# Rests of the kv sums on row halves, one PSUM ring for q and k products, loads as steps of a newly ordered list

## The chip, the cores and the metric

One core of one Trainium2 chip runs the kernel. The metric is the device time of one execution in microseconds (us), as the median of several runs.

## The reference

Linear attention over 8 batches of 8 heads (576 tokens, 64 dimensions) feeds a mixture of 8 experts that picks one expert per token.

```python
def phi(x):                                   # x: q or k, (8, 8, 576, 64)
    proj = np.einsum('bhsd,df->bhsf', x, w_phi)          # 128 features
    proj = proj - np.max(np.abs(proj), axis=-1, keepdims=True)
    return np.concatenate([np.exp(proj), np.exp(-proj)], axis=-1)
kv = np.einsum('bhsf,bhsd->bhfd', k_p, v); z = np.sum(k_p, axis=2)
num = np.einsum('bhsf,bhfd->bhsd', q_p, kv)
den = np.einsum('bhsf,bhf->bhs', q_p, z)[..., None] + 1e-06
...                                           # x = num / den as (4608, 512)
logits = x @ w_gate + modality_bias[modality_id]
e_idx = np.argmax(logits, axis=1)             # one expert per token
...                                           # gate_w: softmax at e_idx
out[mask] = gate_w[mask, None] * (np.maximum(x[mask] @ w1[e], 0.0) @ w2[e])
```

## The kernel before, in words

The work comes in two stages. **Attention** runs over 16 groups `qi` of four heads. Each group goes through the units K, Q, V, T, N and L, and each unit is a Python generator whose `yield`s cut it into steps:

- **K0, K1, K2** (`k`, L550): products of k with w_phi for four, four and one tiles of 128 tokens, two products side by side on the row halves of the array (64 rows, 128 columns of weights; L565); then the largest absolute value (VectorE, L569), the subtraction (L574), two exponentials (ScalarE, L580). The results lie in a PSUM tile of the ring `pk`, which has one slot.
- **Q0, Q1** (`q`, L583): two pairs of products each (L592) into the ring `pq`, also of one slot, a copy each (ScalarE, L596), a maximum over partitions (GpSimd, L600), the subtraction (VectorE, L603), two exponentials (L609).
- **V** (`v`, L612): the kv sums, for the two signs `s` in turn. Of a head's 576 tokens, 512 lie in eight tiles `va` of 128 rows (two row blocks of four); the 64 left over of two heads share one tile, zero-padded in `vb`. The rests (L621) multiply the shared tile with `vb`, 130 columns wide; the main part (L625) is 65 columns wide. Both split the 128 columns of weights into two halves of 64 that run side by side.
- **T** (`t`, L635): four transposes (L641), a copy, products with the gate weights (L650). **N0 to N3, L** (`n`, `l`): numerators and denominators (L676, L695), the division on VectorE, a store of x through SP.

After two `qi` a batch's routing can go on: `xr` and `xl` sum the logits, and **R** (`r`, `Route.group`, L221) finds for four or five tiles of tokens the expert, its weight and the token's place in the expert's list: ten small VectorE operations, a rank product on TensorE (L260, L263), then seven more. **E** and **F** plan the first expert slots from 27 of the 36 tiles.

**Experts** (from p = 0) gather 256 tokens a slot, transpose them, multiply by weights split in a high and a low part (casts L829, L831), and scatter. The first two slots (M, S, MM, SS, L866 and L903) are steps of the same list, with the splits of the weights (W, Y, U); from p = 2 on, `slots` writes fixed code (L883, L885, L903).

**What sets the order.** `ORDER` (L1082) is a written-out list of 1153 steps. TensorE, ScalarE, VectorE and SP take their instructions in the list's order; GpSimd follows dependences and a chain of places (`Line`). Loads aren't in the list: seven stand ahead of it, and `step` (L1187) issues the load for `qi + 2` once the reads of `qi` counted in `READS` have been issued. Ahead of everything, `Numbers`, `Route`, `Attention` and `values` issue their constants: memsets, a running count over 128 columns, a partition number by a product (L99), an identity, 12 and 16 products on ones that keep TensorE at work (L88, L102).

Of the kernel before, what the change touches and what calls it, by code (L numbers as in the profile page):

```python
# [7 lines left out]
F32 = mybir.dt.float32  # L8
# [10 lines left out]
P = 128  # L19
# [18 lines left out]
WARM2 = 16  # L38
# [36 lines left out]
class Numbers:  # L75


    def __init__(self, tc, c, w, ps):
        nc = tc.nc
        self.one = w.tile([P, P], BF16, name="one", bufs=1)  # L80
        nc.vector.memset(self.one, 1.0)

# [3 lines left out]
        pw = ps.tile([P, 512], F32, tag="pm", name="warm")  # L86
        for _ in range(WARM):
            nc.tensor.matmul(pw[:, 0:256], self.one, self.one.unsqueeze(1).to_broadcast([P, 2, P]), start=True, stop=True)  # L88
        self.free = w.tile([P, P], F32, name="free", bufs=1)
        nc.vector.memset(self.free[:, 0:1], 0.0)  # L90
        n = 1
# [3 lines left out]

        mean = w.tile([P, 8], F32, name="mean", bufs=1)
        nc.vector.memset(mean, 1.0 / P)
        pp = ps.tile([P, 512], F32, tag="pm", name="numbers")[:, 0:8]
        nc.tensor.matmul(pp, self.free, mean, start=True, stop=True)  # L99
        pw = ps.tile([P, 512], F32, tag="pm", name="warm2")  # L100
        for _ in range(WARM2):
            nc.tensor.matmul(pw[:, 0:256], self.one, self.one.unsqueeze(1).to_broadcast([P, 2, P]), start=True, stop=True)  # L102
        self.part = w.tile([P, 1], F32, name="partition", bufs=1)
        nc.vector.tensor_copy(self.part, pp[:, 0:1])
        self.ident = c.tile([P, P], F32, name="ident")
        nc.vector.tensor_scalar(self.ident, self.free, self.part, None, ALU.is_equal)
        self.U = w.tile([P, P], BF16, name="U", bufs=1)
        nc.vector.tensor_scalar(self.U, self.free, self.part, None, ALU.is_gt)


class Route:


    def __init__(self, tc, c, w, num, mod, bias, lst):
        self.tc, self.nc, self.lst, self.c, self.w = tc, tc.nc, lst, c, w
        self.listed, self.U = [], num.U
        nc = tc.nc
        self.m2 = w.tile([P, NT, 2], I32, name="m2", bufs=1)
        nc.scalar.dma_start(self.m2, mod.bitcast(I32).rearrange("p (t w) -> p t w", w=2))
        self.bb = w.tile([P, 2, E], F32, name="bb", bufs=1)  # L120
        nc.scalar.dma_start(self.bb, bias.rearrange("m e -> (m e)").partition_broadcast(P)
                            .rearrange("p (m e) -> p m e", m=2))

        self.pad = w.tile([P, E * CAP // P, 2], I32, name="pad", bufs=1)

        self.k = c.tile([P, MOST], F32, name="kf")
        nc.vector.tensor_copy(self.k, num.free[:, 0:MOST])
        self.e = self.k[:, :E]
        self.w8 = c.tile([P, E], F32, name="w8")
        nc.vector.tensor_scalar(self.w8, self.e, -1.0, float(E), ALU.mult, ALU.add)  # L130
        self.ecap = c.tile([P, E], F32, name="ecap")
        nc.vector.tensor_scalar(self.ecap, self.e, float(CAP), None, ALU.mult)
        self.base = c.tile([P, E], F32, name="base")
        nc.vector.tensor_copy(self.base, self.ecap)
        self.k256, self.k32 = (c.tile([P, n], F32, name=f"k{s}") for n, s in ((MOST, 256), (UM, UR)))
        nc.vector.tensor_scalar(self.k256, self.k, 256.0, None, ALU.mult)
        nc.vector.tensor_scalar(self.k32, self.k[:, :UM], float(UR), None, ALU.mult)
        self.row = w.tile([P, P], BF16, name="row", bufs=1)
        nc.vector.tensor_copy(self.row, num.free)
        self.one = num.one  # L140

        self.oh = [c.tile([P, T + 1, E], BF16, name=f"oh{T}") for T in (4, 5)]
        for t in self.oh:
            nc.vector.memset(t, 0.0)

        idf = w.tile([P, NT // 9, 9], F32, name="idf", bufs=1)
        g = w.tile([P, NT // 9], F32, name="first", bufs=1)
        t = w.tile([P, 4], F32, name="tile", bufs=1)
        nc.vector.tensor_scalar(g, num.free[:, 0:NT // 9], 2.0 * S, num.part, ALU.mult, ALU.add)
        nc.vector.tensor_scalar(t, num.free[:, 0:4], float(P), None, ALU.mult)  # L150
        sh = [P, NT // 9, 4]
        nc.vector.tensor_tensor(idf[:, :, 0:4], g.unsqueeze(2).to_broadcast(sh), t.unsqueeze(1).to_broadcast(sh), ALU.add)
        nc.vector.tensor_scalar(idf[:, :, 4:8], idf[:, :, 0:4], float(S), None, ALU.add)
        for j in range(2):
            r = slice(64 * j, 64 * j + 64)
            nc.vector.tensor_scalar(idf[r, :, 8], g[r], float(512 + j * (S - 64)), None, ALU.add)
        self.meta = c.tile([P, NT, 2], F32, name="meta")
        nc.vector.tensor_copy(self.meta.bitcast(I32)[:, :, 1], idf.rearrange("p g t -> p (g t)"))
        self.idf = idf.rearrange("p g t -> p (g t)")[:, :ET]
# [5 lines left out]
        self.me = c.tile([P, 2 * EARLY, 2], I32, name="me")  # L165

# [53 lines left out]

    def group(self, lg, T0, T, pm):  # L221

        nc, w = self.nc, self.w
        sh = [P, T, E]
        n = f"{T0}"
        l = w.tile([P, 5, E], F32, tag="l", name="l" + n)[:, :T]
        nc.vector.tensor_tensor(l, lg, self.bias[:, T0:T0 + T], ALU.add)
        yield
        mx = w.tile([P, 5], F32, tag="mx", name="mx" + n)[:, :T]
# [4 lines left out]
        ex = w.tile([P, 5, E], F32, tag="ex", name="ex" + n)[:, :T]  # L234
# [3 lines left out]
        sc = w.tile([P, 5, E], F32, tag="sc", name="sc" + n)[:, :T]  # L238
# [4 lines left out]
        ohz = self.oh[T - 4]  # L243
# [5 lines left out]
        sm = w.tile([P, 5], F32, tag="sm", name="sm" + n)[:, :T]  # L249
# [29 lines left out]
        lo = self.c.tile([P, 5], I32, tag="lor", name="lor" + n, bufs=2)[:, :T]  # L279
# [4 lines left out]
        for t in range(T0, T0 + T):  # L284
            nc.vector.tensor_scalar(self.low[:, t], self.row, self.lof[:, t:t + 1], None, ALU.is_equal)
# [195 lines left out]
class Attention:  # L481
# [3 lines left out]
    def __init__(self, tc, c, num, w_phi, w_gate):  # L485
        self.tc, self.nc, self.ident = tc, tc.nc, num.ident
        nc = tc.nc
        self.st, self.gs, self.gl, self.lg = {}, {}, {}, {}

        self.wp = c.tile([P, P], F32, name="wp")  # L490
        nc.scalar.dma_start(self.wp[0:64], w_phi)
        nc.scalar.dma_start(self.wp[64:P], w_phi)
        first = c.tile([P, 1], F32, name="first")
        nc.vector.memset(first, 0.0)
        nc.scalar.activation(first, first, AF.Exp)

        self.wgb = c.tile([P, 4, 16], F32, name="wgb")
        nc.vector.memset(self.wgb, 0.0)
        self.wg = w_gate.rearrange("(p j d) e -> j d p e", j=2, d=64)
        self.fold = c.tile([P, 64], F32, name="fold")  # L500
        nc.vector.tensor_tensor(self.fold, self.ident[:, 0:64], self.ident[:, 64:P], ALU.add)

    def values(self, lv):

        nc = self.nc

        self.va = [lv.tile([P, 2, 4, 130], F32, name=f"va{i}") for i in range(2)]
        self.vb = [lv.tile([P, 2, 130], F32, name=f"vb{i}") for i in range(2)]
        for i in range(2):
            nc.vector.memset(self.va[i][:, :, :, 0:130:129], 1.0)  # L510
            nc.vector.memset(self.vb[i], 0.0)
            for j in range(2):
                nc.vector.memset(self.vb[i][64 * j:64 * j + 64, j, 0:130:129], 1.0)
# [6 lines left out]
    def load_q(self, qi, ld, qT, js=(slice(0, 2),)):  # L520
        nc, q = self.nc, self.st.setdefault(qi, {})
        qv = qT[qi].rearrange("p (r a) s -> p a r s", a=2)
        if "qt" not in q:
            q["qt"] = ld.tile([P, 2, S], F32, tag="qt", name=f"qt{qi}")
        for j in js:
            for a in range(2):
                r = slice(64 * a, 64 * a + 64)
                nc.sync.dma_start(q["qt"][r, j], qv[r, a, j])
# [829 lines left out]
```

## Time and profile before

| | us |
|---|---|
| median of 3 runs | 710.33 (710.23 to 710.48) |
| the profiled execution | 710.49 |
| its span, first to last instruction | 708.7 |
| TensorE busy in the span | 695.4 |
| VectorE busy | 555.2 |
| ScalarE busy | 447.1 |
| GpSimd busy | 273.4 |

Engines: PE is TensorE, PEld its weight loads, DVE VectorE, ACT ScalarE, POOL GpSimd, SP the queue that issues most DMAs. A float32 product shows as two records, so a pair of products side by side is four. Ends of matrix products are modelled and overlap the next start, so lengths of TensorE's steps are best read where a chain of waits runs along the engine, from start to start. A line of a chain, as `45.16 0.69 PE pq L592 x4`, is start, length, engine, tile, line of the kernel and number of records.

### The profile page before, as it was taken

To read this page: it belongs to the slowest core of one execution; us is meant where nothing else is said; L and a number is where in the kernel's file an instruction comes from. 1 tells how busy PE (TensorE), PEld (TensorE's weight loads), DVE (VectorE), ACT (ScalarE), POOL (GpSimd) and SP (SyncE) were. 2 spreads that over 40 slices of the span, in tenths; PEclk is the share of its full clock that TensorE was granted. 3 is DMA by queue.
4 is the path that set the end of the run, shared out by engine and by line. 5 is a ranking of instruction groups with operands and counts; after the bars stand their busy time and mean duration, and the time that the engine had idled before them with its cause. 6 is when DMAs were issued, how large, how long until landed. Compare 5 with 4: busy or idle time off the path is not lost.

```text
span 708.7 us, 21200 instructions
## 1 busy us (share of the span) xinstructions
PE 695.4 (98%) x8670; PEld 601.4 (85%) x8670; DVE 555.2 (78%) x1287; ACT 447.1 (63%) x739; POOL 273.4 (39%) x157
## 2 busy tenths in 40 slices
PE   7999999999999999999999999999999999999996
PEld 5889888899898899988888888878888888888885
DVE  7888879899999988679997786678467477578762
ACT  4888688787985884346755575557347357357651
POOL 3555446555545732377733312231231231222021
PEclk9999999999999999999999999999999999999998
DMA  8655555555654658575667549996988983585410
GB/s 231 161 156 162 159 151 152 140 156 158 168 151 127 203 200 283 176 280 176 204 224 290 200 142 412 417 416 224 390 329 336 379 293 132 207 296 191 177 75 28
DMA packets 69705, 155.07 MB, mean 219 GB/s; under 512 B 16090, under 2 KB 44894, under 8 KB 57824
## 3 DMA queue, kind: packets, MB, share of 16 engines
q1 hardware_dynamic: 61920, 134.60, 56.2%
q0 software_dynamic: 7232, 18.92, 7.3%
q8 instruction: 70, 1.15, 0.7%
q14 instruction: 35, 0.29, 0.1%
q10 hardware_dynamic: 448, 0.11, 0.1%
HBM read 134.90 MB, written 19.55 MB: 218 GB/s over the span
## 4 chain that ended last, share of the span: by engine, by line
PE 77%; issue 10%; DVE 5%; POOL 2%; ACT 1%; DMA 1%; SPq 0%; POOLq 0%; ACTq 0%
PE p L903 18%; PE p L883 12%; PE pn L676 9%; PE pv L625 7%; PE p L885 6%; PE pq L592 5%; PE pk L565 4%; PE p L866 3%; DVE l L831 2%; PE pv L621 2%; PE pt L839 2%; PE pt L903 2%; PE pt L1037 1%; PE up L1023 1%; POOL out_dram L791 1%
## 5 line engine op out<-in xcount | busy, mean ns | idle before, releaser
L831 DVE TENSOR_TENSOR l<-raw,h 128x1024 fp32r<-128x1024 f32 x144 | 172.5, 1218 | 5.3 <-ACT h L829 5.2
L600 POOL PARTITION_ALL_REDUCE mq<-d x32 | 131.3, 4103 | 115.1 <-ACT d L596 89.7
L829 ACT CAST h<-raw 128x1024 fp32r<-128x1024 f32 x144 | 145.5, 1051 | 3.7 <-PE pt L903 2.2
L883 PE MATMUL p<-xx,h 128*128 128x512 f32 x512 | 140.2, 395 | 0.0
L886 ACT COPY ts<-p 128x256 f32<-128x256 f32 x128 | 47.8, 373 | 108.6 <-PE p L885 108.6
L903 PE MATMUL p<-h,hh 128*128 128x512 f32 x272 | 107.3, 395 | 0.0
L903 PE MATMUL p<-h,hl 128*128 128x512 f32 x272 | 106.1, 390 | 0.0
L903 PE MATMUL p<-l,hh 128*128 128x512 f32 x272 | 106.0, 390 | 0.0
L883 PEld LDWEIGHTS p<-xx,h 128*128 128x128 f32 x512 | 88.1, 189 | 14.1 <-issue 1.8
L887 DVE TENSOR_TENSOR ts<-ts,p 128x256 f32<-128x256 f32 x128 | 53.5, 418 | 59.1 <-ACT ts L886 59.1
L787 POOL DMA_INDIRECT xg<-x,me x36 | 43.5, 1209 | 141.5 <-PE pt L839 73.1
L791 POOL DMA_INDIRECT out_dram<-os,me x36 | 47.6, 1321 | 124.3 <-DVE os L972 81.3
L885 PEld LDWEIGHTS p<-xx,l 128*128 128x128 f32 x512 | 78.6, 189 | 11.8 <-DVE l L831 0.9
L885 PE MATMUL p<-xx,l 128*128 128x256 f32 x512 | 81.7, 281 | 0.7 <-DVE l L831 0.7
L580 ACT ACTIVATE kp<-dk 128x1024 f32<-128x1024 f32 (+1 forms) x96 | 74.7, 837 | 6.4 <-DVE dk L574 6.4
L676 PE MATMUL pn<-kv,qp 128*64 128x73 f32 x2048 | 73.6, 227 | 0.4 <-DVE kv L653 0.4
L676 PEld LDWEIGHTS pn<-kv,qp 128*64 128x64 f32 x2048 | 68.2, 136 | 5.6 <-issue 2.8
L609 ACT ACTIVATE qp<-d 128x1152 f32<-128x1152 f32 x64 | 71.0, 1160 | 1.6 <-DVE d L603 1.3
L625 PE MATMUL pv<-va,kp 128*64 128x65 f32 x2048 | 70.6, 221 | 0.9 <-issue 0.9
L625 PEld LDWEIGHTS pv<-va,kp 128*64 128x64 f32 x2048 | 68.6, 137 | 1.0 <-issue 1.0
L596 ACT COPY d<-pq 128x576 f32<-128x576 f32 x64 | 40.7, 637 | 32.6 <-PE pq L592 31.6
L889 ACT ACTIVATE hh<-ts 128x256 fp32r<-128x256 f32 x128 | 54.3, 424 | 10.6 <-DVE ts L887 10.3
(240 smaller groups left out, 1101.8 us busy)
## 6 DMA issues: line engine op xcount, KB each, us to landing
raw<-in_w_dram SPq DMA_DIRECT2D x92, 1024.0 KB, 7.6
qt<-in_qT_dram SPq DMA_DIRECT2D x30, 288.0 KB, 4.4
va<-in_vm_dram SPq DMA_DIRECT2D x16, 512.0 KB, 5.0
x<-xs SPq DMA_DIRECT2D x64, 128.0 KB, 3.5
kt<-in_kT_dram SPq DMA_DIRECT2D x15, 512.0 KB, 4.3
kt<-in_kT_dram SPq DMA_DIRECT2D x16, 64.0 KB, 4.7
vb<-in_vt_dram SPq DMA_DIRECT2D x32, 32.0 KB, 4.4
x<-xl SPq DMA_DIRECT2D x32, 32.0 KB, 2.8
```

The lines of the kernel that those rows point to most:

```text
L580: nc.scalar.activation(kp[:, 4 * u:4 * u + T, :, s, :].rearrange("p t a f -> p a t f"), dk, AF.Exp, scale=sc)
L600: self.line.put(nc.gpsimd.partition_all_reduce(mq.rearrange("p a s -> p (a s)"), d.rearrange("p a s -> p (a s)"), P, bass_isa.ReduceOp.abs ...
L609: nc.scalar.activation(qp[:, 2 * pr:2 * pr + 2, i, :], d, AF.Exp, scale=sc)
L625: nc.tensor.matmul(pt[c:c + CW, k // 4, a], kp[:, k, a, s, c:c + CW], va[:, k // 4, k % 4, h], start=False, stop=k == 7, tile_position=(0, c))
L676: nc.tensor.matmul(pp[c:c + CW, g], q["qp"][:, g, s, P * j + c:P * j + c + CW], q["kv"][:, s, g // 2, 73 * (g % 2):73 * (g % 2) + 73], sta ...
L791: ins = self.nc.gpsimd.indirect_dma_start(self.out.rearrange("n (h d) -> (n h) d", d=cols), IndirectOffsetOnAxis(ix.bitcast(U32), 0), o, None,
L829: nc.scalar.copy(h, r)
L831: nc.vector.tensor_tensor(l, r, h, ALU.subtract)
L883: nc.tensor.matmul(pp, h1[:, cc, f], self.XX[:, cc].rearrange("p a t -> p (a t)"), start=cc == 0, stop=False)
L885: nc.tensor.matmul(pp[:, 0:256], l1[:, cc, f], self.XH[:, cc], start=False, stop=cc == 3)
L889: a = nc.scalar.activation(self.HH[:, j], s, AF.Relu)
L903: nc.tensor.matmul(pp, a[:, f, tk], b[:, f], start=i == 0, stop=i == 23)
```

## The change

- The rests: `vb` goes. The leftover 64 rows of each head lie in the ninth tile of `va`, and a product for each row half (64 rows, 128 columns of weights, 65 moving columns) writes its own PSUM tile. The rests of both signs become the first step of V; the main part follows by row block `r`, no longer by sign.
- The ring `pk` goes; `pq` has two slots and serves both k and q.
- `Route.group` takes nine tiles at once: R.3, R.7, R.11 and R.15 are left, and the 27 comparisons that fill `low` become three.
- Constants and set-up become steps (NU, NA, NR); of the products on ones, 12 stay ahead of the list, and PI steps issue four more each, with 64 rows.
- Every load is a step of the list (LP, LA, LB, LK, LQ, LV, LG, LM), on SP except half of w_phi. `READS` goes.
- The list is a new one, of 1200 steps.

```diff
-        for s in range(2):
-            pt = pm.tile([P, 512], F32, tag="pm", name=f"pv{n}_{s}")[:, 0:260].rearrange("p (r a c) -> p r a c", r=2, a=2)
-            for a in range(2):
-                h = slice(65 * a, 65 * a + 65)
-                for c in range(0, P, CW):
-                    nc.tensor.matmul(pt[c:c + CW, :, a], kp[:, 8, a, s, c:c + CW], vb[:, :, h],
-                                     start=True, stop=False, tile_position=(0, c))
...
+        for s in range(2):
+            for a in range(2):
+                for r in range(2):
+                    i = slice(64 * r, 64 * r + 64)
+                    nc.tensor.matmul(pt[r][:, s, a], kp[i, 8, a, s], va[i, 8, 65 * a:65 * a + 65],
+                                     start=s + a == 0, stop=False)
+        yield
+        for r in range(2):
+            for s in range(2):
+                for a in range(2):
+                    for k in range(4):
+                        for c in range(0, P, CW):
+                            nc.tensor.matmul(pt[r][c:c + CW, s, a], kp[:, 4 * r + k, a, s, c:c + CW],
+                                             va[:, 4 * r + k, 65 * a:65 * a + 65],
+                                             start=False, stop=s + a + k == 5, tile_position=(0, c))
+            yield
...
-            pv = [pk.tile([P, 2, 4, P], F32, tag="pk", name=f"pk{n}_{u}")[:, :, 0:T]]
+            pv = [pq.tile([P, 2, 512], F32, tag="pq", name=f"pq{n}_{u}").rearrange("p a (t f) -> p a t f", f=P)[:, :, 0:T]]
...
-        pk = pool(pr, "pk", "right", space=PSUM)
-        pq = pool(pr, "pq", "right", space=PSUM)
+        pq = pool(pr, "pq", "right", bufs=2, space=PSUM)
...
+    def idle(self, n, rows=P):
+        pw = self.ps.tile([P, 512], F32, tag="pm", name="idle")
+        for _ in range(n):
+            self.nc.tensor.matmul(pw[:, 0:256], self.one[:rows], self.one[:rows].unsqueeze(1).to_broadcast([rows, 2, P]), start=True, stop=True)
...
+                if u == "PI":
+                    num.idle(qi, 64)
...
-        for t in range(T0, T0 + T):
-            nc.vector.tensor_scalar(self.low[:, t], self.row, self.lof[:, t:t + 1], None, ALU.is_equal)
+        nc.vector.tensor_tensor(self.low[:, T0:T0 + T], self.row.unsqueeze(1).to_broadcast([P, T, P]),
+                                self.lof[:, T0:T0 + T].unsqueeze(2).to_broadcast([P, T, P]), ALU.is_equal)
```

The new list begins so; behind this stretch, PI.4 stands eight more times (ahead of T.4, between Q1.6 and L.5, between N0.8 and L.8, twice around K0.14, on either side of W1.0 and W3.0, ahead of XV1.0):

```
LA.0 LP.0 NU.0 NU.0 K0.0 NA.0 NA.0 NA.0 NU.0 PI.4 LQ.0 PI.4 Q0.0 LB.0 PI.4 NU.0 Q0.0 PI.4 LK.1 K0.0 K2.0 Q0.0 Q0.0
NA.0 K0.0 Q1.0 K2.0 NU.0 Q1.0 LV.0 K1.0 Q1.0 LG.0 K2.1 NU.0 NU.0 NU.0 NU.0 K2.0 K2.0 K1.0 V.0 Q1.0 K0.0 K0.1 K1.0
K1.0 NU.0 LQ.1 V.0 V.0 Q0.0 V.0 K2.1 K0.1 K0.1 K1.1 LV.1 K2.1 Q0.0 LK.2 K0.1 K1.1 Q1.0 NU.0 Q0.1 NU.0 K2.1 K1.1 Q0.0
LV.2 V.0 V.1 V.1 T.0 ...
```

## Rows read from the trace of the kernel before

**Rows 1.** The page's busy time of TensorE, its share of the span, its instructions

```profile
PE 695.4 (98%) x8670; PEld 601.4 (85%) x8670; DVE 555.2 (78%) x1287; ACT 447.1 (63%) x739; POOL 273.4 (39%) x157
```

**Rows 2.** Busy time by stage: PE, PEld, DVE, ACT, POOL, granted clock, DMA share, GB/s

```profile
0.00:10.00 10.00, 8.56 (x54) 6.13 (x56) 5.82 (x44) 1.49 (x2) 2.16 (x9) 1.00 0.71 206
10.00:20.00 10.00, 7.49 (x110) 5.44 (x108) 9.93 (x11) 8.30 (x12) 7.18 (x2) 1.00 1.13 273
...
80.00:100.00 20.00, 19.07 (x457) 17.03 (x455) 14.96 (x34) 15.86 (x24) 8.25 (x3) 1.00 0.48 134
100.00:120.00 20.00, 19.67 (x460) 17.65 (x458) 18.77 (x64) 16.52 (x25) 12.15 (x3) 1.00 0.52 143
220.00:240.00 20.00, 19.62 (x453) 16.91 (x448) 19.70 (x63) 14.87 (x21) 15.07 (x6) 1.00 0.45 127
260.00:280.00 20.00, 19.72 (x261) 19.04 (x262) 16.25 (x36) 11.61 (x17) 6.06 (x6) 1.00 0.95 338
```

**Rows 3.** The chain of waits, 290 to 420 us

```profile
300.68 0.14 PE rk L263 x10
...
312.75 0.91 PE p L883 x4
...
371.88 10.93 PE p L903 x48
...
394.89 10.93 PE p L903 x48
```

**Rows 4.** The chain of waits along TensorE, 44 to 63 us

```profile
45.16 0.69 PE pq L592 x4
...
46.89 0.49 PE pq L592 x4
...
53.06 0.22 PE pk L565 x4
53.28 0.37 PE pv L621 x4
53.66 0.93 PE pv L625 x32
54.59 0.23 PE pv L621 x4
...
56.43 0.89 PE pk L565 x16
...
60.37 0.43 PE kvT L650 x16
```

**Rows 5.** TensorE's weight loads by line and shape, before 312 us

```profile
L625 PEld LDWEIGHTS pv<-va,kp 128*64 128x64 f32 x2048 | 68.6, 137 | 1.0 <-issue 1.0
...
L565 PEld LDWEIGHTS pk<-wp,kt 64*128 64x128 f32 x576 | 38.3, 188 | 9.1 <-issue 2.5 <-DVE dk L574 1.7 <-PE pq L592 1.6
```

**Rows 6.** TensorE in order of time, before 24 us: start, length, group

```profile
4.62 3.57 PE L102 MATMUL warm<-one 128*128 128x256 bf16 x16
8.13 1.65 PE L565 MATMUL pk<-wp,kt 64*128 64x128 f32 x20
...
23.50 0.76 PE L592 MATMUL pq<-qt,wp 64*128 64x288 f32 x4
```

**Rows 7.** DMA issues: number, KB each, median us to landing

```profile
kt<-in_kT_dram SPq DMA_DIRECT2D x2, 256.0 KB, 3.2
...
wp<-in_w_phi_dram ACTq DMA_DIRECT2D x2, 32.0 KB, 3.1
```

**Rows 8.** VectorE by line and shape, before 312 us: busy us, mean ns

```profile
L574 DVE TENSOR_TENSOR dk<-pk,mk 128x1024 f32<-128x1024 f32 x31 | 37.8, 1220 | 0.9
...
L230 DVE TENSOR_REDUCE mx<-l 128x5 f32<-128x40 f32 x4 | 0.8, 196 | 0.1
```

**Rows 9.** ScalarE by line and shape, before 312 us

```profile
L580 ACT ACTIVATE kp<-dk 128x1024 f32<-128x1024 f32 x64 | 63.8, 1051 | 4.9 <-DVE dk L574 4.8
```

**Rows 10.** What TensorE waited for before 312 us: total, times, longest

```profile
PE pq L592 <- ACT d L596: 1.7, 2, 0.9
```

More of the change, by code (lines that the diff above doesn't have):

```diff
@@ L37 @@
 WARM = 12
-WARM2 = 16
 UR, US, UM = 32, 5, 8
@@ L85, in __init__, with ops @@
         nc.gpsimd.partition_all_reduce(m, z, P, bass_isa.ReduceOp.absmax)
[L86 to L89, printed above, removed]
+        self.idle(WARM)
+    def ops(self):
+        nc, w = self.nc, self.w
         nc.vector.memset(self.free[:, 0:1], 0.0)
+        yield
         n = 1
@@ L94, in __init__ @@
             n *= 2
+            yield
         mean = w.tile([P, 8], F32, name="mean", bufs=1)
         nc.vector.memset(mean, 1.0 / P)
-        pp = ps.tile([P, 512], F32, tag="pm", name="numbers")[:, 0:8]
+        yield
+        pp = self.ps.tile([P, 512], F32, tag="pm", name="numbers")[:, 0:8]
         nc.tensor.matmul(pp, self.free, mean, start=True, stop=True)
-        pw = ps.tile([P, 512], F32, tag="pm", name="warm2")
-        for _ in range(WARM2):
-            nc.tensor.matmul(pw[:, 0:256], self.one, self.one.unsqueeze(1).to_broadcast([P, 2, P]), start=True, stop=True)
@@ L134, in __init__ @@
-        nc.vector.tensor_copy(self.base, self.ecap)
+        self.w8, self.ecap, self.base = (c.tile([P, E], F32, name=n) for n in ("w8", "ecap", "base"))
         self.k256, self.k32 = (c.tile([P, n], F32, name=f"k{s}") for n, s in ((MOST, 256), (UM, UR)))
-        nc.vector.tensor_scalar(self.k256, self.k, 256.0, None, ALU.mult)
-        nc.vector.tensor_scalar(self.k32, self.k[:, :UM], float(UR), None, ALU.mult)
         self.row = w.tile([P, P], BF16, name="row", bufs=1)
-        nc.vector.tensor_copy(self.row, num.free)
@@ L140, in __init__ @@
[L140 to L156, printed above, removed]
+        self.oh = c.tile([P, 10, E], BF16, name="oh")
+        self.idf3 = w.tile([P, NT // 9, 9], F32, name="idf", bufs=1)
@@ L1237, in leave @@
                 room()
-            if u not in ("SU", "E", "F", "XG", "WL00", "WL01") and ex.PT is None:
+            if u not in ("NU", "NA", "NR", "SU", "E", "F", "XG", "WL00", "WL01") and ex.PT is None:
                 feat.close()
@@ L1286, in first @@
                 yield from ex.wparts(k)
[L1288 removed]
+        own = ("PI", "NU", "NA", "NR", "SU", "E", "F", "XG", "WL", "TU", "TV", "TW", "XS", "XV", "XW", "M", "MM", "S", "SS", "W", "Y", "U")
         p1, ex.PT = [], None
         with tc.manual_schedule(engines={SP, PE, ACT, DVE}):
[L1291 to L1299 removed]
+            num.begin()
             for o in ORDER:
```

335 lines of the change are left out of this document (180 added, 155 removed).

## The prediction

> **What bounds the kernel now.** I read the page's busy shares first, then the table by stage, then TensorE's own order of work. TensorE is busy for 98% of the span [rows 1]. The table by stage [rows 2] shows where the list leaves it idle: in the first 20 us, and in a few tenths after 80 us. The engine was busy and not waiting everywhere else, VectorE included: it reaches 19.70 of 20 us in 220 to 240, so it is the engine that comes next. The list ends where the first wide expert product starts, at 312.75 us [rows 3]; from there every expert slot costs 23.0 us (371.88 to 394.89), and the change touches nothing behind that point. So the time is the list's length on TensorE plus some 398 us, and I cost the change by what it does to that length: the steps' own columns, the changes of the array's shape between steps, and the waits.
>
> The steps have fixed lengths, read off the chain of waits as it runs along TensorE [rows 4]: a product of q 0.49 us, a large one of k 0.89, a small one of k 0.22, half of a kv sum 2 x (0.23 + 0.93) = 2.32. They grow where the array's shape changes: q costs 0.69 when it stands between products with 64 columns of weights and 0.49 behind k, and the rest of a kv sum 0.37 behind k and 0.23 behind its like. I take 0.2 us for a change into the 64-row shape and 0.15 for one out of it, 0.175 as a mean.
>
> **The change, part by part.** The sum is made against the profiled execution (span 708.7, time 710.49, so 1.8 around the span); it stands 0.16 above the median of 710.33.
>
> *Rests of the kv sums.* Before, the 16 sums have 4 pairs of products each, 130 columns wide over a zero-padded tile, 0.23 us a pair (four records, two for each float32 product). After, they have 4 pairs over row halves, 65 columns wide, but with weights of 64 rows x 128 columns instead of 128 x 64. Is such a pair paced by its moving columns or by its weights? At the pace of the columns it costs what a pair of the main part does, 0.93/8 = 0.116 us [rows 4]. For the weights: L650 moves only 16 columns and still needs 0.43 us for 16 records [rows 4], 0.108 for a pair, nearly as long as a pair with 65; so 64 columns of weights set that pace. The weight load of 128 columns takes 188 ns and that of 64 columns 137 [rows 5], 51 ns less, and the small k product (a pair on row halves, 128 columns of weights) takes 0.22 [rows 4]. So I take 0.22 a pair, the row nearest in shape: 64 x (0.23 - 0.22) = 0.6 us less, taken as 0.5. The other end is 0.116: 64 x 0.114 = 7.3 less. The upper end is none.
> The Trainium skill says otherwise: TensorEngine Tiling (Array Packing), Theoretical Speedup, promises up to twice the rate where the contracted dimension is 64 or less. By that rule the pair would cost half. No product in this trace has 64 rows and as few as 65 moving columns, so it is a rival below.
> The main part keeps its 64 products per sum in another order.
>
> *Changes of shape.* I marked each TensorE step of both lists as 64-row (q, k, new rests, fillers), 64-column (kv sums, numerators, folds, ranks) or full (transposes, experts), and counted neighbours that differ: 117 before, 105 after, the new rests and fillers included. 12 x 0.175 = 2.1 us less. Bounds: 1.8 and 2.4 by the two prices.
>
> *Start.* Before, the first real product runs at 8.13 us and the first 23.5 us hold 4 large k (3.56), 1 small (0.22), 5 q (2.45) and both halves of V.0 (4.64), 10.9 us of work [rows 4, 6]: 12.6 us lost. After, the first half of k (256 KB) is issued first, about 0.75, and such a load lands in 3.2 us; w_phi is next, 3.1 us [rows 7]; so K0.0 runs at about 4.5. The 16 warm-up products before 8.13 us cost 3.57/16 = 0.223 us for 256 columns [rows 6], the 1.2 GHz level by their length, though the table prints 1.00; I let that level last until such work has run for as long as before, about 8.7 us, so K0.0 takes 1.8. Then VectorE decides: K0.0's maximum and subtraction (1.22 + 1.22 [rows 8]; two exponentials of 1.05 each follow on ScalarE [rows 9]), the small ones, and K1.0's, which needs LB.0 and stands behind q and four fillers. By these lengths K1.0's exponentials land at 16.6, V.0 ends at 20.1 instead of 23.5, and at 24.6, ahead of T.0, TensorE has done 13.8 us of steps: 10.8 lost. 1.9 us less. Bounds: 3.6 less (the whole lead of the first product is kept) and nothing (VectorE's chain is as long as before). What moves into the list besides: some 33 set-up operations of VectorE that ran before 7 us for nothing, 5.6 us at about 0.17; the numbers' product on TensorE (0.2, in the walk); ScalarE's first exponential; GpSimd's three memsets and the list's clearing store on SP, 1.7 us on a queue that is idle between its reductions; the loads of modality and bias, from ScalarE's queue to SP's. None of these but the product is on TensorE, and I cost them there at nothing: their readers, the ranks, come after four of the sixteen groups.
>
> *Fillers.* 12 PI steps of four 256-column bf16 products. The first four lie in the wait for loads and are in the walk above. The other eight stand among steps that, by the trace, leave no hole: at the 2.4 GHz level 256 columns are 0.107 (half of the 1.2 GHz level's), so 8 x 4 x 0.107 = 3.4 us more. Bounds: none (each lies in a wait) and 3.4.
>
> *Ranks on nine tiles.* TensorE issues 80 products instead of 88, of some 14 ns each (0.14 us for ten [rows 3]): nothing. VectorE issues the fifteen small operations of a group 4 times instead of 8, 60 x 0.19 = 11.4 us less [rows 8]. The 27 row comparisons of 128 elements become 3 of 1152, much the same work. With the 5.6 moved in, VectorE has some 6 us less to do inside the list.
>
> *One PSUM ring, loads as steps.* k and q now share two slots; nothing is added, but a k product can wait for a q copy, and q for k's subtraction. Before, with one slot each, q waited 1.7 us for its own copy in all, in two waits of up to 0.9 [rows 10]. A load step on SP can hold the x stores behind it; the loads stand ten and more TensorE steps ahead of their readers, and the k load and w_phi land in 3.2 us [rows 7], so I cost it at nothing. If that cover went, a late load would cost its whole delay.
>
> *Waits after 24 us.* The table lacks 0.93 + 0.33 + 0.38 + 0.28 = 1.9 us of TensorE between 80 and 280 [rows 2]. With VectorE, at up to 19.7 of 20 us there, relieved of 6 us I take 1.5 less; bounds 1.9 less and, since new waits can be as long as the new list makes them, several us more (the rival).
>
> **Sum:** -0.5 - 2.1 - 1.9 + 3.4 - 1.5 = -2.6 us: 707.9 for the profiled run, 707.7 against the median. With the fillers free 704.3; with start and waits giving nothing 711.1. That is this case's own range.
>
> **Rivals.**
> *The rests go at half price.* For it: row halves surely run side by side (the k pair's 0.22 for two products). Against it: the 0.108 of L650 and the 188 against 137 ns. Another 6.8 us: 700.9. Chance 0.14.
> *No change.* The new list meets waits of its own in place of the old ones, and start and shapes are eaten by the fillers: -0.5 - 2.1 - 1.9 + 3.4 + 1 = 0 or so, 710.2. The searched list is then not better, only other. For it: TensorE was 98% busy, so there was little to find. Chance 0.23.
> *Slower: the nine-tile ranks.* R.3, R.7, R.11 and R.15 each have ten small VectorE operations, one upon the other, ahead of the rank product on TensorE, and now all nine tiles wait for one chain; behind the product stand q, k and numerators. Ten at 0.19 to 0.23 are some 2 us if VectorE does nothing between them, and it is nearly full there. By walking the new list with these lengths I get waits of about 1.7 us at three of the four: 5.2 us, 712.9. It decides against the change once the four cost more than 2.6 + 1.4 = 4 us together, 1 us each. For it: VectorE's 19.70 of 20. Against it: the old list had eight such chains and TensorE shows no wait for a rank. Chance 0.17.
>
> **How the numbers follow.** 0.2%, 1.42 us, is about what a measurement of this kernel can tell from no change. Faster: my forecast, 0.46, and the half-price rests, 0.14, 0.60 together. Within: 0.23. Slower: 0.17. The range goes from 700.5 (half-price rests) to 712.5 (most of the rank waits), and leaves out a list that starves or gains by more.
>
> **What would show it.** The pairs of rests at 0.22 (right) or 0.12 (the rival); the first real product at 4.5 us and V.0's end near 20; the first wide product at about 310; PI steps of 0.43 with TensorE busy on both sides (right) or idle time around them; waits of TensorE before the rank products. I am wrong if the list ends before 307 with the rests at 0.22, or if the expert slots stop being 23.0 us.

## The result, and the profile after

The changed kernel takes 718.43 us (median of 6 runs, 715.03 to 719.71), the kernel before 710.52 beside it (6 runs, 710.23 to 711.17): ratio 1.0106, 95% interval 1.0083 to 1.013 (the medians alone stand at 1.0111). It is slower by 7.9 us, well beyond the 0.2% that counts here, where I had forecast 707.7 and faster. It also scatters five times as much.

The page of the profiled run (719.71 us), against [rows 1]: TensorE is as busy as before, VectorE has 9 us less to do, and the span is 9.2 us longer.

```profile
span 717.9 us, 21115 instructions
PE 695.1 (97%) x8694; PEld 604.3 (84%) x8694; DVE 546.2 (76%) x1195; ACT 445.6 (62%) x735; POOL 280.3 (39%) x157
```

The table by stage, columns as in [rows 2]:

```profile
0.00:10.00 10.00, 7.91 (x58) 5.77 (x60) 3.94 (x16) 2.12 (x3) 0.66 (x6) 1.00 0.82 214
10.00:20.00 10.00, 7.59 (x170) 7.12 (x168) 7.61 (x14) 9.72 (x15) 7.87 (x2) 1.00 0.93 215
...
80.00:100.00 20.00, 19.43 (x438) 17.18 (x435) 16.07 (x42) 15.51 (x25) 8.94 (x3) 1.00 0.43 114
100.00:120.00 20.00, 20.00 (x484) 18.58 (x480) 17.68 (x55) 15.21 (x22) 10.45 (x3) 1.00 0.73 200
220.00:240.00 20.00, 17.26 (x409) 15.06 (x408) 19.38 (x54) 10.38 (x16) 7.36 (x2) 1.00 0.24 65
260.00:280.00 20.00, 17.04 (x296) 15.87 (x293) 13.91 (x38) 11.79 (x14) 2.20 (x3) 1.00 0.88 310
```

Between 80 and 120 us nothing is amiss. In 220 to 240 and 260 to 280 us TensorE has 17.26 and 17.04 of 20, where before had 19.62 and 19.72. The chain of waits gives the end of the list, and two starts of expert slots:

```profile
310.49 10.91 PE p L935 x48
321.39 0.91 PE p L915 x4
...
403.69 10.95 PE p L935 x48
...
426.71 5.49 PE p L935 x24
```

The first wide product starts at 321.39 us (312.75 before, [rows 3]), 8.6 us later; a slot is still 23.0 us (403.69 to 426.71), and from the first wide product to the end of the span it is 396.5 us against 396.0. Nearly all of the loss is in the list. What TensorE waited for there, from 24 to 322 us, has no main culprit (total, times, longest):

```profile
PE pn L710 <- issue: 2.2, 2, 1.6
PE pn L710 <- DVE gs L701: 1.3, 2, 0.8
PE pn L710 <- DVE rd L695: 1.1, 1, 1.1
PE pn L710 <- ACT h L861: 1.0, 1, 1.0
PE pl L729 <- DVE kv L687: 0.9, 1, 0.9
...
PE rk L287 <- DVE oh L272: 0.4, 1, 0.4
```

This view lists 10.2 us of waits in all, and 2.0 us for the kernel before; as ends of products are modelled and overlap the next start, it sees only a part. So I kept accounts. TensorE's records of each trace were laid against the steps of the list; each step got its length by the prediction's prices ([rows 4], with the price of a change of shape), and what it took beyond that is its wait. The column of the steps' work is thus priced and not measured, and a wrong price would show as a wait; from 100 to 160 us after keeps 0.3 us beyond the prices and before 1.4, so they fit there. The sums, in us, by the stretch in which the step began (sums of other runs stand in the text where they are used):

| kernel | to 24 | 24 to 100 | 100 to 160 | 160 to 204 | 204 to 250 | 250 to 280 | behind | steps' work | V.0 ends | list ends |
|---|---|---|---|---|---|---|---|---|---|---|
| before | 4.3 | 2.2 | 1.4 | 0.6 | 1.1 | 1.0 | 0.1 | 293.9 | 23.5 | 312.6 |
| after | 4.9 | 2.5 | 0.3 | 2.8 | 5.7 | 4.0 | 0.2 | 296.9 | 20.8 | 321.2 |
| after, again | 6.4 | 1.9 | 0.5 | 3.0 | 6.0 | 3.1 | 0.2 | 296.9 | 21.5 | 321.9 |
| no late reductions | 2.7 | 2.8 | 0.6 | 2.8 | 0.8 | 5.9 | 0.2 | 296.9 | 18.6 | 316.5 |
| no late fillers | 3.1 | 2.5 | 0.5 | 2.8 | 8.0 | 3.7 | 0.7 | 293.0 | 19.1 | 318.4 |
| old tail from 854 | 3.2 | 1.7 | 0.4 | 3.6 | 8.4 | 1.6 | 0.2 | 295.3 | 19.5 | 318.7 |
| plan early | 5.6 | 1.7 | 0.7 | 2.8 | 9.9 | 6.0 | 0.2 | 296.9 | 21.6 | 327.7 |
| old list, new code (e1b) | 14.4 | 6.5 | 4.3 | 0.8 | 1.8 | 1.7 | 0.2 | 297.6 | 34.9 | 330.9 |

List end = first real product (8.13 before, 4.08 after) + work + waits. The waits behind 160 us are 2.7 before and 12.7 after: that is where 10 us were lost. Two profiles of after agree within 0.02 us from V.0's end to the list's end (300.41 and 300.39), so what differs between its executions here is the start.

For the last of these stretches the chain of waits in after shows one piece that the chain of before does not have: a store of x that lands 9.56 us after its issue, on the queue SP, 1.4 us behind two weight loads of 1 MB. VectorE waits for the buffer that it frees (chain; issues on SP; VectorE's wait):

```profile
255.02 9.56 DMA x<-xs
```

```profile
253.65 1.22 SPq L842 DMA_DIRECT2D raw<-in_w_dram  x2
255.02 1.95 SPq L718 DMA_DIRECT2D x<-xs  x2
```

```profile
DVE xs L699 <- DMA x<-xs: 1.8, 1, 1.8
```

The second profile of after has it too (9.26 us, a wait of 1.5). No run moved these loads alone, so its share of the loss is not known; it is not all of it, as two runs below have no such wait and still 5.9 and 6.0 us of TensorE's from 250 to 280 us.

### The profile page after: what moved, and what is told of

Its sections match the earlier page's. It is cut to its first block, busy times and chain, and to the rows that moved or that the text cites. A ratio compares the mean times of both kernels' runs of the same rounds, so it can differ in the third digit from the quotient of the medians.

```text
span 717.9 us, 21115 instructions
## 1 busy us (share of the span) xinstructions
PE 695.1 (97%) x8694; PEld 604.3 (84%) x8694; DVE 546.2 (76%) x1195; ACT 445.6 (62%) x735; POOL 280.3 (39%) x157
## 4 chain that ended last, share of the span: by engine, by line
PE 64%; DVE 11%; issue 10%; DMA 2%; POOL 2%; ACT 0%; SPq 0%; POOLq 0%; DVEq 0%
PE p L935 18%; PE p L915 12%; PE p L917 6%; PE pn L710 5%; PE pv L658 4%; PE p L898 3%; PE pq L620 3%; PE pk L593 3%; DVE l L863 2%; PE pt L871 2%; PE pt L935 2%; DMA x<-xs 1%; DVE mk L597 1%; POOL out_dram L823 1%; PE pt L1069 1%
## 5 line engine op out<-in xcount | busy, mean ns | idle before, releaser
L819 POOL DMA_INDIRECT xg<-x,me x36 | 48.2, 1339 | 154.7 <-PE pt L871 72.2
L823 POOL DMA_INDIRECT out_dram<-os,me x36 | 49.8, 1384 | 118.2 <-DVE os L1004 76.0
L710 PE MATMUL pn<-kv,qp 128*64 128x73 f32 x2048 | 75.3, 228 | 6.4 <-issue 2.2
L658 PE MATMUL pv<-va,kp 128*64 128x65 f32 x2048 | 65.5, 222 | 2.4 <-issue 2.4
L658 PEld LDWEIGHTS pv<-va,kp 128*64 128x64 f32 x2048 | 62.4, 138 | 4.8 <-issue 3.7
L597 DVE TENSOR_REDUCE mk<-pk 128x8 f32<-128x1024 f32 (+3 forms) x50 | 45.4, 917 | 21.5 <-PE pk L593 21.4
L921 ACT ACTIVATE hh<-ts 128x256 fp32r<-128x256 f32 x128 | 54.3, 424 | 10.8 <-DVE ts L919 10.6
```

The costliest lines, as they stand in the source:

```text
L658: nc.tensor.matmul(pt[r][c:c + CW, s, a], kp[:, 4 * r + k, a, s, c:c + CW], va[:, 4 * r + k, 65 * a:65 * a + 65], start=False, stop=s + a ...
L710: nc.tensor.matmul(pp[c:c + CW, g], q["qp"][:, g, s, P * j + c:P * j + c + CW], q["kv"][:, s, g // 2, 73 * (g % 2):73 * (g % 2) + 73], sta ...
L823: ins = self.nc.gpsimd.indirect_dma_start(self.out.rearrange("n (h d) -> (n h) d", d=cols), IndirectOffsetOnAxis(ix.bitcast(U32), 0), o, None,
L921: a = nc.scalar.activation(self.HH[:, j], s, AF.Relu)
```

## The experiments

Ratios are to the kernel before on the same chip. On one chip before takes 720 us itself; six runs, named below, were made there, and before has no profile on it. On the other chips it takes 710 us, and the accounts compare only profiles from these.

**After once more**, unedited, as the yardstick.

> The changed kernel itself, once more, on the chip of the runs beside it, since an earlier chip gave 720 us for the kernel before. Ratio to before 1.008 to 1.013; the list ends within 4 us of the recorded 321.2, and its waits of TensorE (20.3 us in the recorded profile) differ from execution to execution by as much as its times do (715 to 720).

Ratio 1.0124 (1.0097 to 1.015); the list ends at 321.91, with 21.0 us of waits. As expected.

**No late reductions: are the waits locks?** VectorE in after, in order of time (start, length, line, operation), then GpSimd's reductions:

```profile
215.02 0.22 DVE L268 TENSOR_REDUCE mx<-sc 128x9 f32<-128x72 f32 x1
215.28 2.21 DVE L272 TENSOR_TENSOR oh<-sc,mx 128x72 bf16<-128x72 f32 x1
217.41 0.22 DVE L277 TENSOR_REDUCE sm<-ex 128x9 f32<-128x72 f32 x1
217.55 1.38 DVE L307 TENSOR_SCALAR lor<-de 128x9 int32<-128x9 int32 x1
...
230.87 1.91 DVE L386 TENSOR_TENSOR g3e<-g2e,kf 128x48 f32<-128x48 f32 x1
237.37 1.67 DVE L389 TENSOR_SCALAR ote<-ote 128x6 f32<-128x6 f32 x1
250.80 1.32 DVE L370 TENSOR_SCALAR me<-ids 128x12 int32<-128x12 f32 x1
```

```profile
214.47 4.43 POOL L628 PARTITION_ALL_REDUCE mq<-d  x1 [3.39 <-ACT d L624]
230.28 3.94 POOL L628 PARTITION_ALL_REDUCE mq<-d  x1 [11.38 <-ACT d L624]
236.58 3.94 POOL L628 PARTITION_ALL_REDUCE mq<-d  x1 [2.37 <-ACT d L624]
```

```diff
-        self.line.put(nc.gpsimd.partition_all_reduce(mq..., d..., P, absmax))
+        if qi < 13:
+            self.line.put(nc.gpsimd.partition_all_reduce(mq..., d..., P, absmax))
...
-        nc.vector.tensor_tensor(d, d, mq, ALU.subtract)
+        nc.vector.tensor_tensor(d, d, mq if qi < 13 else <column of the identity, broadcast>, ALU.subtract)
```

> After with the six reductions across partitions on GpSimd left out that belong to q of the last three heads; a column of the identity is subtracted in their place, by an operation of the same shape, so these heads' features and the experts of the last tiles are others; only the list is compared. Theory LOCKS: operations of VectorE that start while such a reduction runs wait for a part of it; in the recorded profile five operations of the rank and route chain between 215 and 252 us took 2.21, 1.38, 1.90, 1.67 and 1.32 us, where the same operations take 0.16 to 0.39 elsewhere, 7.3 us in all, and that stage is the one where TensorE waits. Then these five take their short times and the first wide product starts 5 to 8 us earlier than in after. Rival ORDER ALONE (the waits come from where the steps stand, with or without the locks): it starts less than 2 us earlier.

The same operations, and the stage:

```profile
213.61 0.23 DVE L272 TENSOR_TENSOR oh<-sc,mx 128x72 bf16<-128x72 f32 x1
213.90 0.16 DVE L307 TENSOR_SCALAR lor<-de 128x9 int32<-128x9 int32 x1
...
231.43 0.17 DVE L389 TENSOR_SCALAR ote<-ote 128x6 f32<-128x6 f32 x1
```

```profile
220.00:240.00 20.00, 20.00 (x472) 18.05 (x470) 18.33 (x69) 14.09 (x21) 0.00 (x0) 1.00 0.37 99
260.00:280.00 20.00, 18.05 (x239) 17.81 (x236) 12.81 (x27) 8.21 (x11) 4.58 (x3) 0.91 0.81 292
```

The long operations are short, and the waits of 204 to 250 us fall from 5.7 to 0.8. From 204 to 280 us VectorE in after waits for no reduction's result, so these were locks: operations held off while a reduction ran. The list ends 4.7 to 5.4 us earlier, at the lower edge of the 5 to 8 that were expected, but 2.2 to 2.9 of that is this run's start (V.0 ends at 18.6). From V.0's end on it is 297.9 against 300.4, only 2.5 us, little more than the 2 that the rival allows: of the 4.9 us of waits that went, 1.9 came back between 250 and 280 us (4.0 to 5.9).

**The old list under the new code: is it the code?** Pools as before (one slot each for k and q), set-up steps and early loads at the head, before's steps behind; a kv sum's rests stand right ahead of its first main step, R.1, R.5, R.9 and R.13 fall away.

```diff
-        pq = pool(pr, "pq", "right", bufs=2, space=PSUM)
+        pq = pool(pr, "pq", "right", bufs=1, space=PSUM)
...
-            pv = [pq.tile([P, 2, 512], F32, tag="pq", ...
+            pv = [pq.tile([P, 2, 512], F32, tag="pk", ...
...
+    LP.0 LA.0 LB.0 LQ.0 LM.0 LK.1 LV.0 LQ.1 NU.0 (x10) PI.4 (x4) NU.0 (x3) NA.0 (x5) LG.0 LV.1 LM.1 NR.0 (x15)
+    K2.0 K2.0 SU.0 SU.0 K0.0 K0.0 Q0.0 Q0.0 K2.0 K1.0 LK.2 Q0.0 ...
```

> The code of after (rests on row halves, nine-tile ranks, set-up operations and loads as steps) under the list of before: the set-up steps, four fillers and the loads stand at the head, later loads stand where before issued them, a k product and a q product have one PSUM slot each as before. Theory ORDER (the 9 us that the list of after lost to waits come from the order of its steps): the waits of before return, the rests cost 0.3 to 0.5 less, but 129 changes of shape stand against 117, 12 x 0.175 = 2.1 more: 711.5 to 713. Rival RANKS (chains over nine tiles, and comparisons of 1152 elements in one instruction, make VectorE late wherever they stand): 715 or more.

> The same, with the PSUM ring of after: k and q products share two slots. ORDER: within 0.7 us of the run with one slot each, 711.5 to 713. Rival RING (a product of k waits for a copy of q and the other way round, wherever the steps stand): over 2 us slower than that run.

In these two the head cleared the gates' tile behind its load, so the gate weights were zero and the experts unevenly filled; they took 746 and 749 us, on the chip where before takes 720, and are not read.

> The code of after under the list of before, again, with the head mended: loads of modality and bias early, the gates after their tile is cleared, one PSUM slot each for k and q. Theory ORDER: 129 changes of shape against 117 cost 2.1, the rests give 0.3 to 0.5 back, and a kv sum now holds two PSUM slots from its rests on, which may make it wait for a numerator at some sums: ratio to before 1.002 to 1.006 (712 to 714.5 where before has 710.5). Rival RANKS: 1.010 or more, with waits of TensorE before or behind the rank products.

This run is e1b in the table. Ratio 1.0332 (1.0309 to 1.0356), far over both expectations, in part for a reason of my own making: VectorE stood for 8.8 us, because the clearing of a value tile's edge columns came behind that tile's load, TensorE waited for it, and V.0 ends at 34.9. (The next pair moves another set-up step instead, so its start waits in the same way.) What can be read is behind that:

```profile
200.00:220.00 20.00, 20.00 (x476) 18.47 (x476) 18.74 (x50) 16.52 (x23) 10.70 (x3) 1.00 0.51 142
220.00:240.00 20.00, 20.00 (x498) 17.96 (x496) 17.86 (x69) 12.86 (x19) 7.88 (x2) 1.00 0.46 125
240.00:260.00 20.00, 19.18 (x434) 16.76 (x432) 19.43 (x51) 15.65 (x21) 16.70 (x6) 1.00 0.54 143
```

From 160 us on it waits 4.5 us, not 12.7, and at no rank product: the nine-tile chains, rests and loads as steps don't make waits of that size under every list. From 24 to 160 us it waits 10.8 (3.6 before); a part of that is still the start, but the code has its part:

```profile
PE pv L650 <- DVE gs L701: 1.9, 3, 1.0
PE pv L650 <- DVE rd L697: 0.8, 1, 0.8
```

A kv sum now takes two PSUM buffers with its rests, where the old one took one at a time, and waits until a numerator's reader has freed the second. The list ends 18.3 us later than before's (330.9 against 312.6), and V.0's end accounts for 11.4 of them; so the new code loses about 6.9 us more under the old list, against the 8.6 that after loses in all.

> The code of after under the list of before, the two first set-up steps of the route moved to where before has the third, loads in the order of before. By the earlier run the stretch behind 160 us is short of TensorE's waits (4.5 us against 2.7 in before and 12.7 in after), that from 24 to 160 us has kv sums that wait for a second PSUM slot (about 5 us at six sums), and 12 more changes of shape cost 2.1. With a head like before's: list end 312.6 + 2.1 + 5 + 1.8 = 321 or so, ratio to before 1.009 to 1.015. If the rank chains over nine tiles cost anything, TensorE waits ahead of the rank products, and the ratio is above that.

> The same with the shared ring of two slots. RING FREE: within 1.5 us of the run beside it. RING COSTS: more than 2 us slower, with waits of a k product for a q product or for the subtraction of another k.

Both on the chip where before takes 720: 744.94 and 744.69, ratios 1.0311 (1.0265 to 1.0357) and 1.0339 (1.0301 to 1.0377). Both are over the 1.009 to 1.015 expected, and the head still made VectorE wait for the value load. What the pair tells is the difference: the list ends at 343.5 and 344.0, so the shared ring costs at most some 0.5 us under this list. But it also waits late: from V.0's end to the list's end it takes 310.8 and 311.5 us, e1b 296.0. A part of that goes with the chip, on which after without late fillers takes 307.8 us for this and 299.3 on another. Another part is locks that e1b does not have: at 239.63 and 244.96 us (first of the pair) two operations of VectorE of one form take 2.95 and 2.55 us, in place of 0.71 in e1b, both inside a reduction. So the old list keeps the new code from late waits in e1b, and not in every run.

**The new start before the old list.** The first 66 steps of the new list, then before's.

> The first 66 steps of the list of after, then the steps of the list of before that are left, in their order, with the set-up steps that are left spread over the next 130 steps; shared PSUM ring, no late fillers. ORDER (of the later part): the start of after is worth what it showed, 1.9 to 2.7 us against the same code under the list of before, so 709 to 711. Rival START (the new start leaves VectorE or the loads behind for the rest of the list): 713 or more.

740.12 on the chip where before takes 720, ratio 1.0274 (1.024 to 1.0308): the set-up steps that I spread stood too close behind the modality load (TensorE waited 6.3 us for a kv copy behind them, and its granted clock was 0.83 from 40 to 60 us).

> The first 66 steps of after's list, then what is left of the list of before, the loads of modality and bias early, the set-up steps spread. ORDER: 2 to 3 us less than the run under the list of before alone, ratio 0.999 to 1.003. Rival START (what the new start leaves for later costs as much as it saves): no less than that run.

728.32, ratio 1.0266 (1.0226 to 1.0305). V.0 ends at 19.5, as after's start promises, but 24 to 100 us cost 10.9 us of waits: set-up operations that now stand there meet reductions (one took 2.40 us in place of 0.17, another 2.23 in place of 0.30), and the kv sums wait for PSUM. Behind 160 us it waits 4.8, like e1b, and this one has the shared ring. The expectations of both were wrong: a start can't be put before another list for nothing.

**The old tail behind the new list.**

```diff
     ... V.12 XL.11 XL.11 V.12 N1.11                  (the first 854 steps of after)
-    SU.0 V.12 XR.11 R.11 R.11 K2.14 K2.14 R.11 LV.14 Q1.13 V.13 ...
+    SU.0 R.7 R.7 R.7 LK.15 XR.11 R.11 R.11 R.11 R.11 R.11 ...   (what is left of before's list)
```

> The first 854 of the 1200 steps of after's list (up to some 204 us), then what is left of the list of before, in its order; code of after. TensorE's own work between the plan's product (E) and the first expert product (M0) is 20.0 us in after's list, 32.2 in before's and 32.3 here. Theory PLAN LATE (after 204 us the list of after leaves the route plan, and the weights it names, too little cover, and locks on VectorE stretch that chain): the waits behind 204 us fall from 9.8 us to 2 to 3.5, five fillers fewer and three changes of shape more make 1.6 less work, and the first wide product starts at 311.5 to 315, ratio to before 1.000 to 1.006. Rival EARLY PART (the first 204 us leave the rest short of something, whatever the order behind): 318 or later, 1.009 or more.

716.95, ratio 1.0097 (1.0077 to 1.0117), and the list ends at 318.7: both as the rival EARLY PART had it, and outside PLAN LATE. The waits of 250 to 280 us do go (4.0 to 1.6), as PLAN LATE said, but those of 204 to 250 grow to 8.4, at the seam (TensorE in order of time, then the stage):

```profile
209.01 2.06 PE L658 MATMUL pv<-va,kp 128*64 128x65 f32 x64
214.09 0.28 PE L287 MATMUL rk<-oh,U 128*64 128x80 bf16 x2 [3.02 <-DVE oh L272]
```

```profile
200.00:220.00 20.00, 16.90 (x332) 15.14 (x327) 17.92 (x74) 11.09 (x15) 8.01 (x2) 0.84 0.66 180
220.00:240.00 20.00, 19.64 (x446) 17.45 (x446) 17.21 (x48) 11.41 (x17) 9.35 (x3) 0.90 0.34 89
```

Here the rank chain over nine tiles has nothing beside it: TensorE stands for 3.0 us, and its granted clock is 0.84 and 0.90 in the two stages around it. These waits are not locks: behind 160 us no VectorE operation of this run takes 0.4 us more than its shortest like, and TensorE still waits 13.8 us there.

> The same without the three fillers between 80 and 204 us. FILLERS ON THE PATH: 3 x 0.43 = 1.3 us less than the run with them. FILLERS IN WAITS: the same within 0.4.

713.97, ratio 1.0058 (1.0036 to 1.008), the best of the changed kernels: 3.0 us less than with the three fillers, of which 1.3 is theirs by their length; from V.0's end on it is 1.7 us, and the rest is the start.

> Like the first of these, but the list of before takes over at step 747 (some 180 us), before the waits that after shows at 185 us (1.3) and behind it. PLAN LATE with its neighbours: the waits from 160 to 204 us fall from 2.8 to about 1 us, 1 to 2 us less than the first of these. Rival: the sums under the list of before wait for PSUM (1.0 to 1.4 us at three of them in the runs under that list alone), and nothing is won.

719.81, ratio 1.012 (1.0096 to 1.0144): the seam is 20 us earlier and costs as much there (8.1 us from 160 to 204). Nothing is won.

> The old list behind step 854 without late fillers, where a product of k, a transpose and the first half of a kv sum now stand ahead of the rank product of group 11, so that TensorE does not run dry during the seven small operations of the nine-tile chain. The wait of 3.2 to 3.4 us at the seam goes, and with it the lower clock behind it (0.91 in 220 to 240 us): first wide product 312.5 to 314, ratio to before 0.999 to 1.002, level with before. If the new start were worth nothing, 1.004 or more.

719.48, ratio 1.0144 (1.0128 to 1.0159). The wait ahead of the rank product is gone, and 10.0 us of waits stand in 204 to 250 us at the next steps (3.1 behind T.12, 2.4 behind T.13). The expectation was wrong: the work on VectorE that the wait covered still has to be done.

**The plan alone, early.** The steps R.11, E, F, XG and the first two weight loads, moved up to where before has them behind the last logits; all else as in after.

> After's own list with the steps of the plan alone moved (the ranks of group 11, the early plan, its parts, the first gather, the first two weight loads): they stand as many microseconds of TensorE's work behind the last logits of group 11 as in before's list. TensorE's work between the plan's product and the first expert product: 35.4 us where after has 20.0. Nothing else moves and all fillers stay. Theory PLAN LATE: the waits of 250 to 280 us fall from 3.1 to 4.0 to under 2, those of 204 to 250 from 5.7 to 6.0 to 4 or less as the locks fall elsewhere; first wide product 316 to 318.5, ratio to before 1.004 to 1.008. Rival ORDER OF THE REST: waits behind 204 us stay at 9 us or more, and the ratio at 1.010 or more.

724.75, ratio 1.0213 (1.0199 to 1.0227). TensorE in order of time, and the stages:

```profile
216.15 1.16 PE L593 MATMUL pk<-wp,kt 64*128 64x128 f32 x16
220.56 2.08 PE L593 MATMUL pk<-wp,kt 64*128 64x128 f32 x16 [3.25 <-DVE dk L602]
```

```profile
200.00:220.00 20.00, 15.89 (x382) 14.39 (x378) 18.67 (x63) 12.63 (x18) 12.06 (x3) 1.00 0.64 183
220.00:240.00 20.00, 17.11 (x388) 15.32 (x390) 18.36 (x56) 10.35 (x15) 0.62 (x2) 0.91 0.15 35
```

PLAN LATE falls: with more cover the waits rise to 9.9 and 6.0. VectorE does the plan sooner, and k stands behind it: its product waits 3.25 us for the subtraction that frees a slot of the shared ring. One of the plan's operations ahead of that subtraction takes 2.31 us (at 216.34) in place of 0.16, inside a reduction. Whether a slot of its own would have helped k, no run shows: in before, where k has one, its product waits for this subtraction too (0.8 us, at the start).

> The same without the eight late fillers: 3.4 less if they stand on the path (by the run without them alone they are worth 1 to 3), first wide product 313.5 to 317, ratio 1.001 to 1.006. If a wait then lowers TensorE's granted clock, it is not below the run with fillers.

721.90, ratio 1.0181 (1.0167 to 1.0195), far over the 1.001 to 1.006 expected: 2.9 us less than with fillers, and slower than after as well.

**Without the eight late fillers.**

```diff
-    ... V.4 K2.5 PI.4 T.4 ...        (and seven more PI.4 behind it)
+    ... V.4 K2.5 T.4 ...
```

> After without the eight late fillers (the four of the first 10 us stay). If they stand on the path, as the prediction took it: 8 x 0.43 = 3.4 less, 715.0. ORDER, in its strong form (TensorE waits for VectorE there anyway): about 1 us less or nothing, 717 to 718.5. Rival FILLERS HELP (the later waits come from elsewhere, and a filler keeps nothing but the clock): slower than after with a granted clock below 1.00 around 260 to 290 us.

> After without its eight late fillers, once more, on another chip than the first time. FILLERS ON THE PATH: 3.4 less than after, ratio to before 1.006 to 1.008 where after has 1.0106 and 1.0124. FILLERS IN WAITS: 1.010 to 1.013. FILLERS HELP: above 1.013, with a granted clock under 1.00 behind 260 us, as the first time.

Ratios 1.0094 (1.0061 to 1.0127) on the 720 us chip, 1.0093 (1.0072 to 1.0114) on the other, where after has 1.0106 and 1.0124: 1 to 2 us less, between the two theories of the second run. From V.0's end on it is 299.3 against 300.4: of the 3.4 us of filler work 1.1 is won, 2.3 is waits again (204 to 250 us: 5.7 to 8.0), with a lower granted clock there:

```profile
220.00:240.00 20.00, 16.74 (x360) 14.78 (x362) 19.55 (x58) 10.05 (x14) 7.96 (x2) 0.91 0.31 85
```

In after that stage has 1.00. No version beat the kernel before.

## Why the prediction was wrong, step by step

The step that failed is the term "Waits after 24 us", -1.5, with the bound "several us more" left to a rival. By the accounts these waits went from 6.3 to 15.4, +9.1. The other terms hold in sum: first product and start -1.8 (8.13 + 4.3 against 4.08 + 4.9 + 1.7 of fillers; forecast -1.9, though its own 12.6 - 10.8 is 1.8), the steps' work +1.3 with the fillers of the start taken out (forecast +0.8). -1.8 + 1.3 + 9.1 = 8.6, the measured shift of the list's end. The work stands at the prediction's own prices; no run measured the changes of shape alone.

*Why I took the waits for small.* I reasoned from sums: VectorE has 6 us less to do, so TensorE waits less. VectorE did get 9 us less, and the waits more than doubled. The base was too small as well: I took the 1.9 us that the table lacks for all of before's waits, where the accounts have 6.3, and VectorE for busy throughout, where [rows 2] has it at 14.96 of 20 in 80 to 100. As far as the runs show, the waits depend on which VectorE operation stands ahead of which, in an in-order list, in a stage where VectorE is hardly idle (19.38 of 20), and on which of them meet a reduction on GpSimd; from 260 to 280 us, where VectorE has only 13.91 of 20, that does not explain them. I took a busy VectorE for a working one; in after's 19.38, 3.2 us are the excess of the two long operations at 230.87 and 237.37.

*Rests: right.* TensorE in order of time at the start of after:

```profile
4.08 1.76 PE L593 MATMUL pk<-wp,kt 64*128 64x128 f32 x16 [0.27 <-DMA wp<-in_w_phi_dram]
...
12.00 1.01 PE L650 MATMUL pv<-va,kp 64*128 64x65 f32 x16
12.85 1.11 PE L593 MATMUL pk<-wp,kt 64*128 64x128 f32 x16
...
14.21 3.25 PE L658 MATMUL pv<-va,kp 128*64 128x65 f32 x102
19.86 1.03 PE L658 MATMUL pv<-va,kp 128*64 128x65 f32 x26 [2.40 <-issue]
```

Four pairs from 12.00 to 12.85, 0.21 each: paced by 128 columns of weights, as forecast with 0.22. The rival at half price falls, and with it, for fp32 with 65 moving columns, the gain that the Trainium skill, TensorEngine Tiling (Array Packing), Theoretical Speedup, allows at most. What I missed of them is the second PSUM buffer.

*Start: right, in part by luck.* First real product 4.08 (4.5), V.0's end 20.8 (20.1). But V.0 stops for 2.40 us in its middle (the line at 19.86), which the forecast did not have; without that stop it would have ended at some 18.4, 1.7 us ahead of the forecast.

*Fillers: a third of the price.* I charged 3.4; taking them out gives 1.1 behind the start. They stand partly in waits, which I took as a bound; in the list with the plan early they cost 2.9.

*Ranks, ring, loads at nothing: right under the old list in e1b* (no wait at a rank product) and in the pair (ring free within 0.5 us), and not shown elsewhere: at a seam without cover the chain costs 3.0 us, with the plan early k waits 3.25 us for a slot, and in after a store of x lands late behind weight loads. The prediction named that store, and priced it at nothing. The rival "nine-tile ranks" had the right sign by the wrong mechanism: TensorE's wait before rank products is 0.4 us in all, not 5.2.

*Expert slots: right*, 23.0 us.

What is shown: on the chips where before takes 710 us the new code under the old order has late waits of 4.5 and 4.8 us, not 12.7 (e1b, and the new start before the old list), so the late loss goes with the order; and 4.9 us of after's waits in 204 to 250 us are locks, of which removing the reductions wins 2.5 at the list's end. What stays open: why the code waits late under the old list on the other chip; a cause for the waits of 160 to 204 us, which every list with the new middle part shows (1.5 to 3.6 us; 8.1 where the seam lies in it); what the late store of x costs; and which part of the order behind 204 us would have to change, as moving the plan, the tail or the seam only moved the waits.

## What to carry to other kernels

When two in-order engines are both near full, don't price a new order of work by sums per engine: lay out which operation waits behind which, stage by stage, or give the waits a range as wide as the stage's slack is small. Before counting an engine as busy, compare each operation with the shortest of its form: an excess that lies inside a reduction on GpSimd is lock time, and it moves with the order. It is no measure of TensorE's waits, though: the run with the old tail has none of it late, and waits as long. In this kernel no piece of one list could be set into the other without waits of its own.

## What the runs showed of the hardware that was not expected

*A reduction across partitions holds some VectorE operations off, in two parts.* In after, operations with two inputs in SBUF, or scalar operations on one, that started 0.1 to 1.5 us into a reduction of 3.94 us ended 2.46 to 2.52 us into it, and 3.0 into one of 4.43. Most others in the same windows took their usual time: a VectorE reduction of a tile in SBUF 0.57 us into one took 0.19 us (at 237.15), and operations that read PSUM took theirs unless they stood behind a held one. Scalar operations that started 3.1 and 3.35 us into reductions of 4.43 and 4.65 ended with them, while additions of two SBUF tiles at 3.0 and 3.7 took their usual 0.22. The Trainium skill, SBUF — State Buffer, SBUF: two separate sides, has a VectorE operation with two inputs in SBUF, or in a two-port mode, and a GpSimd operation that reads SBUF exclude each other for a whole instruction. The rows agree that such operations wait; that they go on within the reduction, and not only at its end, is new. Whether the lock is let go, or the reduction is several accesses, no run shows.

*TensorE stops for nothing in the middle of a sum.* In all thirteen profiles with this start V.0 stops behind record 102 of the 128 of its main part ("issue" above), always the same one, for 0.4 to 2.7 us; before has no such stop. A 16 KB packet of the instruction queue ends 1.3 to 1.6 us before TensorE goes on, each time, amid the loads: in four of them it ends at 16.30, 17.07, 18.33 and 18.43, and TensorE goes on at 17.64, 18.55, 19.81 and 19.86 us. So TensorE probably waited for its instructions; no run took the loads away. V.0's end lies between 18.4 and 21.6 us over these profiles, a spread of 3.2 us; the times of after's own executions spread by 4.7.

*The clock around a wait.* After, whose longest wait is 2.4 us in its start and 1.6 later, has a granted clock of 1.00 in every stage from 20 to 320 us, the level of 2.4 GHz. Stages in or behind a wait of about 3 us show less, a mean that lies between this level and that of 1.2 GHz: 0.84 and 0.90 at the seam, 0.91 with the plan early. But shorter waits go with it as well: 0.91 from 260 to 280 us without late reductions, where the longest wait that the view lists is 1.9 us, and 0.91 from 220 to 240 without late fillers, where it is also 1.9.
